# First input blocks and V weights on two DMA queues, one block's norm sums on ScalarE, the first block scaled in halves, the last two stores in another order

## The chip, the core and the metric

The kernel runs on one core of a Trainium2 chip. A core has TensorE (PE, matmuls; PEld is its loading of weights), VectorE (DVE), ScalarE (ACT), GpSimd (POOL) and SyncE (SP). Each runs its own list of instructions in a fixed order and waits for others through semaphores. SP and ACT can issue DMA transfers, each on a queue of its own. The metric is the device time of one execution in microseconds (us); five runs of the kernel before lie between 279.61 and 280.01, with a median of 279.67.

## The reference

Input `x` is 2048 rows of 512 in bf16. It is layer-normed; the normed rows feed an attention with a sliding window (32 heads of 16, each row sees itself and the 255 rows before it) and a gated product of width 1792. The output is the sum of `x` and both.

```python
xn = layernorm(x)                                   # mean and variance of each row, eps 1e-5
q, k, v = split(xn @ wqkv)                          # 32 heads, 16 wide
p = softmax(where(0 <= i - j < 256, q @ k.T * 0.25, -1e9))
a = (p @ v) @ wo
g = ((xn @ w_gate) * (xn @ w_up)) @ w_down
return x + a + g
```

## The kernel before

The 2048 rows are 16 blocks of 128 rows, four blocks to a chunk, so four chunks. `run` (L424) first calls `setup` and `first_chunk`, and then walks through 96 steps of scores (`scores`, L214: S = K Q on PE, exponential on ACT, masks on POOL). After each step it puts as many pieces of other PE work as a running account of costs allows: projections of the next chunk, gate and up products, down products, output products. The order of every engine's instructions follows from the order of these calls; nothing is reordered later. A wait is put in wherever an instruction reads what another engine wrote.

`setup` (L49) issues all loads on SP's queue, in this order: x block 0, x block 1, x blocks 2 and 3 together (L61 and L62), the three column groups of the weights for V, K and Q (L63 and L64), halves of the gate and up weights with x blocks 4 to 7 between, then the down and output weights and the rest of x. A transfer counts on one of eight completion counters in turn; the ninth waits until the counter it takes is free. ACT meanwhile loads its function table and runs one exponential on a 128x1 tile (L77). PE runs 42 products of a unit matrix (L87), whose result is not used.

`first_chunk` (L190) norms the blocks of chunk 0. For a block:

- `norm_stats` (L110): DVE makes the statistics of 512 columns (`st`, L116) and turns them into mean and variance (`mv`, L117).
- `norm_scale` (L120): POOL adds eps (`ve`, L125) and raises to the power -0.5 (`rs`, L127), both on 128x1.
- `norm_apply` (L131): DVE subtracts the mean and multiplies by `rs`, which gives `xn` (L135). The `xn` tiles come from a ring of four buffers.
- `norm_transpose` (L139): PE transposes `xn` in four pieces of 128 columns (`xTp`, L151), and ACT copies them to `xnT` (L152).
- `proj_v` (L160): four products of `xnT` with V's weights on PE (`vp`, L165), copied to `V` by ACT (L169).

In the kernel before DVE's order is: statistics of blocks 0 and 1, scaling of 0, statistics of 2, scaling of 1, statistics of 3, scaling of 2, scaling of 3. PE's order is: transposes of 0, of 1, V product of 0, transposes of 2, V product of 1, transposes of 3, V products of 2 and 3, then the first K and Q products (L177). ACT's order is `xnT` of 0 and 1, V of 0, `xnT` of 2, V of 1, `xnT` of 3, V of 2 and 3.

At the end the sum of the last block (chunk 3, block 3) lies as two halves of 256 columns in two banks of one PSUM tile, `psd3`. `wo` (L320) runs its last eight products, four for the first half and four for the second; in the second half a product with a unit matrix has already added `x` (`add_x`, L325). `store` (L331) drains a half: the second by a copy on ACT, stored from ACT's queue; the first by an addition of `x` on DVE, stored from SP's queue. Before the change the second half's `store` is called first (L485), then the first half's (L486).

Of the kernel before, what the change touches and what calls it, by code (L numbers as in the profile page):

```python
# [7 lines left out]
BF16 = mybir.dt.bfloat16  # L8
F32 = mybir.dt.float32
I32 = mybir.dt.int32  # L10
ACT = mybir.ActivationFunctionType
ALU = mybir.AluOpType
# [10 lines left out]
class Kernel:  # L23
# [25 lines left out]
    def setup(self):  # L49
        nc, const, NT, NF = self.nc, self.const, self.NT, self.NF  # L50
        self.x = const.tile([128, NT, 512], BF16, name="x")
        self.Wqkv = const.tile([128, 4, 1536], BF16, name="Wqkv")
        self.Wo = const.tile([128, 4, 512], BF16, name="Wo")
        self.Wg = const.tile([128, 4, self.F], BF16, name="Wg")
        self.Wu = const.tile([128, 4, self.F], BF16, name="Wu")
        self.Wd = const.tile([128, NF, 512], BF16, name="Wd")
        xv = self.x_d.rearrange("(t p) d -> p t d", p=128)
        wq = self.w_d["qkv"].rearrange("(k p) n -> p k n", p=128)
        wg = self.w_d["g"].rearrange("(k p) n -> p k n", p=128)
        wu = self.w_d["u"].rearrange("(k p) n -> p k n", p=128)  # L60
        for lo, hi in ((0, 1), (1, 2), (2, 4)):  # L61
            nc.sync.dma_start(out=self.x[:, lo:hi, :], in_=xv[:, lo:hi, :])  # L62
        for lo in (1024, 512, 0):  # L63
            nc.sync.dma_start(out=self.Wqkv[:, :, lo:lo + 512], in_=wq[:, :, lo:lo + 512])  # L64
        h = self.F // 2
        for lo in (0, h):
            nc.sync.dma_start(out=self.Wg[:, :, lo:lo + h], in_=wg[:, :, lo:lo + h])
            nc.sync.dma_start(out=self.Wu[:, :, lo:lo + h], in_=wu[:, :, lo:lo + h])
            if lo == 0:
                nc.sync.dma_start(out=self.x[:, 4:8, :], in_=xv[:, 4:8, :])  # L70
        nc.sync.dma_start(out=self.Wd[:], in_=self.w_d["d"].rearrange("(f p) n -> p f n", p=128))
        nc.sync.dma_start(out=self.Wo[:], in_=self.w_d["o"].rearrange("(c p) n -> p c n", p=128))
        nc.sync.dma_start(out=self.x[:, 8:NT, :], in_=xv[:, 8:NT, :])

        warm = const.tile([128, 1], F32, name="warm")
        nc.vector.memset(warm[:], 0.0)
        nc.scalar.activation(out=warm[:], in_=warm[:], func=ACT.Exp)  # L77
        ident = const.tile([128, 128], BF16, name="ident")
        nc.gpsimd.memset(ident[:], 0.0)
        nc.gpsimd.affine_select(out=ident[:], in_=ident[:], compare_op=ALU.not_equal, fill=1.0,  # L80
                                base=0, pattern=[[-1, 128]], channel_multiplier=1)
        self.ident = ident
        self.accb = self.ps_a.tile([128, 512], F32, name="accb")
        nc.vector.memset(self.accb[:], 0.0)
        wps = self.ps_m.tile([128, 128], F32, tag="M", name="wps")
        for _ in range(42):
            nc.tensor.matmul(wps[:], lhsT=ident[:], rhs=ident[:], start=True, stop=True)  # L87
        pi = const.tile([128, 1], I32, name="pi")
        nc.gpsimd.iota(pi[:], pattern=[[0, 1]], base=0, channel_multiplier=1)
        podd = const.tile([128, 1], I32, name="podd")  # L90
        nc.vector.tensor_scalar(out=podd[:], in0=pi[:], scalar1=4, scalar2=1,
                                op0=ALU.arith_shift_right, op1=ALU.bitwise_and)
        self.odd = const.tile([128, 1], F32, name="odd")
        nc.vector.tensor_copy(out=self.odd[:], in_=podd[:])
        self.mhalf = const.tile([128, 4], F32, name="mhalf")
        nc.gpsimd.memset(self.mhalf[:], -0.5)
        self.xnT, self.Q, self.hT, self.O, self.OT = {}, {}, {}, {}, {}
        self.K, self.Ko, self.V = {}, {}, {}
        self.strips, self.at = {}, {}
# [20 lines left out]
    def norm_scale(self, t, n=4):  # L120
# [7 lines left out]
        for u in range(t, t + n):  # L128
            self.stats[u][2] = rs

    def norm_apply(self, t):  # L131
        nc = self.nc
        mv, j, rs = self.stats.pop(t)
        xn = self.xpool.tile([128, 512], BF16, tag="xn", name="xn")
        nc.vector.tensor_scalar(out=xn[:], in0=self.x[:, t, :], scalar1=mv[:, j, 0:1],  # L135
                                scalar2=rs[:, j:j + 1], op0=ALU.subtract, op1=ALU.mult)
        self.xns[t] = xn

    def norm_transpose(self, t, by_dma):  # L139

        nc = self.nc
        xn = self.xns.pop(t)
        T, b = divmod(t, 4)
        if b == 0:
            self.xnT[T] = self.chunk2.tile([128, 4, 4, 128], BF16, tag="xnT", name=f"xnT{T}")
        if by_dma:
            nc.sync.dma_start_transpose(out=self.xnT[T][:, b, :, :], in_=xn[:])
            return
        ps = self.ps_m.tile([128, 4, 128], BF16, tag="M", name="xTp")
        for k in range(4):  # L150
            nc.tensor.transpose(ps[:, k, :], xn[:, 128 * k:128 * k + 128], self.ident[:])  # L151
        nc.scalar.activation(out=self.xnT[T][:, b, :, :], in_=ps[:], func=ACT.Copy)  # L152

    def bank(self, ks, name):

# [34 lines left out]
    def first_chunk(self):  # L190

        self.new_chunk(0)
        for b in range(2):
            self.norm_stats(b, 1)
            self.norm_scale(b, 1)
        for b in range(4):
            self.norm_apply(b)
            if b < 2:
                self.norm_stats(b + 2, 1)
                self.norm_scale(b + 2, 1)  # L200
        self.norm_transpose(0, False)
        for b in range(4):
            if b < 3:
                self.norm_transpose(b + 1, False)
            self.proj_v(b)
        self.proj_qk(0, 0, 1)
        self.proj_qk(0, 0, 0, on_act=True)
        self.proj_qk(0, 1, 1)
# [215 lines left out]
    def run(self):  # L424
# [49 lines left out]
        T = NCH - 1  # L474
# [7 lines left out]
        fill(10 ** 9, -1)  # L482
        assert n == len(work)
        self.wo(T, 3, (0, 1, 2, 3))
        self.store(T, 3, 1, True)  # L485
        self.store(T, 3, 0)  # L486


@with_exitstack
# [34 lines left out]
```

## Time and profile before

| | |
|---|---|
| median of five runs | 279.67 us (279.61 to 280.01) |
| the profiled execution, its own time | 279.66 us |
| its span, first to last instruction | 277.9 us |
| busy: PE, DVE, ACT, POOL | 269.1, 188.2, 183.1, 164.4 us |
| granted TensorE clock, mean | 0.999 of full speed |
| first x block landed, first statistics | 2.92 us |
| first transposes of block 0 on PE | 5.32 us |
| first V product | 6.85 us |
| first K product | 11.01 us |
| last matmuls issued from | 273.12 us, for 1.04 us |
| last store issued | 275.06 us |

The span is shorter than the time by 1.76 us, which lies around the first and the last instruction. A line of the timeline gives start and length in us, the engine, the line of the kernel, what is written and read, the shapes, and in brackets how long the engine was idle before it and what released it. `SPq` and `ACTq` are DMA issues of SP and ACT; their length is the time that the issue took, and how long a transfer took to land stands with the DMA issues. Matmuls are pipelined, so that one PE line can start before the one before it has ended.

### The profile page before, as it was taken

The page shows a single profiled execution, that of the slowest core. Times are in us where ns is not written, and L with a number is a line of the kernel's source. Part 1 is how long each engine was busy: PE and PEld are TensorE (multiplying, and loading weights), DVE is VectorE, ACT ScalarE, POOL GpSimd, SP SyncE. Part 2 cuts the span into 40 slices and gives each one's busy share as a digit, 9 for nine tenths or more (in the row PEclk, how much of TensorE's full clock was granted, in tenths as well). Part 3 has the DMA queues.
Part 4 walks back from the last instruction along what each step waited for, and adds up shares of the span by engine and source line. Part 5 has one row for each costly group of instructions (what it writes and reads, how often), then busy time and mean ns, then how long its engine had stood idle before and what let it go on. Part 6 is the DMA issues. An engine that isn't in the chain of part 4 may idle for free.

```text
span 277.9 us, 5829 instructions
## 1 busy us (share of the span) xinstructions
PE 269.1 (97%) x2396; PEld 114.4 (41%) x2414; DVE 188.2 (68%) x338; ACT 183.1 (66%) x121; POOL 164.4 (59%) x284
## 2 busy tenths in 40 slices
PE   6999999999999999999999999999999999999994
PEld 6433333334344444344444344444434444433453
DVE  6387989788567777858855778774853477777232
ACT  3666766786767666688666676769676766767601
POOL 4146666765786756574877656575656566656510
PEclk9999999999999999999999999999999999999999
DMA  7999411000112100000012200000001000000002
GB/s 215 375 371 349 110 21 21 19 0 2 39 40 57 21 2 0 1 2 0 2 40 59 55 2 2 0 2 1 0 2 40 19 21 1 2 0 2 0 2 75
DMA packets 17162, 13.74 MB, mean 49 GB/s; under 512 B 7024, under 2 KB 17136, under 8 KB 17136
## 3 DMA queue, kind: packets, MB, share of 16 engines
q1 hardware_dynamic: 16848, 13.18, 15.5%
q8 instruction: 19, 0.31, 0.5%
q10 hardware_dynamic: 288, 0.20, 0.2%
q14 instruction: 7, 0.06, 0.1%
HBM read 9.70 MB, written 2.10 MB: 42 GB/s over the span
## 4 chain that ended last, share of the span: by engine, by line
PE 87%; ACT 5%; DVE 3%; issue 1%; POOL 1%; DMA 1%; ACTq 0%; DVEq 0%
PE psd L317 18%; PE up L300 17%; PE gp L289 17%; PE S L223 11%; PE qkp L177 9%; PE accb L256 7%; PE psd L323 5%; ACT P L231 4%; PE vp L165 3%; ACT V L169 1%; DMA x<-in_A_x_dram 1%; DVE st L116 1%; DVE gsb L294 1%; DVE xn L135 1%; DVE hT L304 0%
## 5 line engine op out<-in xcount | busy, mean ns | idle before, releaser
L231 ACT ACTIVATE P<-S 128x2048 bf16<-128x2048 f32 (+2 forms) x96 | 170.0, 1771 | 74.3 <-PE S L223 62.6
L236 POOL TENSOR_SCALAR_AFFINE_SELECT P<-P 128x512 bf16<-128x512 bf16 x128 | 84.7, 662 | 54.3 <-ACT P L231 54.2
L240 POOL TENSOR_SCALAR_AFFINE_SELECT P<-P 128x512 bf16<-128x512 bf16 x112 | 72.5, 647 | 38.3 <-ACT P L231 38.3
L300 PE MATMUL up<-xnT,Wu 128*128 128x512 bf16 x224 | 60.0, 380 | 0.1
L289 PE MATMUL gp<-xnT,Wg 128*128 128x512 bf16 x224 | 59.7, 380 | 0.0
L317 PE MATMUL psd<-Wd,hT 128*128 128x512 bf16 (+1 forms) x225 | 52.3, 366 | 1.4 <-issue 1.1
L263 DVE STREAM_TRANSPOSE at<-accb 128x512 f32<-128x512 f32 x32 | 22.8, 714 | 39.0 <-PE accb L256 39.0
L304 DVE TENSOR_TENSOR hT<-up,gsb 128x512 bf16<-128x512 f32 x56 | 38.1, 681 | 7.8 <-PE up L300 5.8
L294 DVE CAST gsb<-gp 128x512 bf16<-128x512 f32 x56 | 37.9, 677 | 5.9 <-PE gp L289 5.8
L317 PEld LDWEIGHTS <-hT 128*128 128x128 bf16 x238 | 21.5, 98 | 24.9 <-issue 4.7
L289 PEld LDWEIGHTS <-Wg 128*128 128x128 bf16 x224 | 20.0, 97 | 26.1 <-issue 5.2
L177 PE MATMUL qkp<-xnT,Wqkv 128*128 128x512 bf16 x128 | 30.6, 380 | 0.0
L300 PEld LDWEIGHTS <-Wu 128*128 128x128 bf16 x224 | 19.6, 97 | 26.4 <-issue 7.1
L256 PE MATMUL accb<-P,V 128*17 128x384 bf16 (+2 forms) x704 | 25.4, 276 | 0.0
L341 DVE TENSOR_TENSOR y<-psd,x 128x512 bf16<-128x512 f32 (+1 forms) x15 | 9.9, 667 | 17.9 <-PE psd L323 16.5
L223 PE MATMUL S<-Q,K 16*128 16x256 bf16 (+2 forms) x352 | 18.4, 276 | 0.5
L223 PE MATMUL S<-Q,Ko 32*128 32x256 bf16 (+2 forms) x352 | 18.4, 275 | 0.4 <-ACT P L231 0.2
L276 DVE TENSOR_TENSOR on<-at,rz 128x256 bf16<-128x256 f32 x32 | 18.1, 566 | 0.4
L177 PEld LDWEIGHTS <-Wqkv 128*128 128x128 bf16 x128 | 11.4, 98 | 14.6 <-issue 2.7
L256 PEld LDWEIGHTS <-V 128*17 128x17 bf16 x704 | 13.8, 90 | 8.7 <-issue 5.3
L182 DVE CAST K<-qkp 128x512 bf16<-128x512 f32 x16 | 11.0, 689 | 9.0 <-PE qkp L177 8.7
L323 PE MATMUL psd<-Wo,OT 128*128 128x512 bf16 (+1 forms) x67 | 16.6, 367 | 0.2 <-issue 0.2
(39 smaller groups left out, 140.1 us busy)
## 6 DMA issues: line engine op xcount, KB each, us to landing
Wg<-in_B_w_gate_dram SPq DMA_DIRECT2D x2, 896.0 KB, 10.3
Wu<-in_B_w_up_dram SPq DMA_DIRECT2D x2, 896.0 KB, 11.5
Wd<-in_B_w_down_dram SPq DMA_DIRECT2D x1, 1792.0 KB, 15.5
out_dram<-y SPq DMA_DIRECT2D x14, 128.0 KB, 1.7
Wqkv<-in_A_wqkv_dram SPq DMA_DIRECT2D x3, 512.0 KB, 5.8
x<-in_A_x_dram SPq DMA_DIRECT2D x1, 1024.0 KB, 10.4
x<-in_A_x_dram SPq DMA_DIRECT2D x1, 512.0 KB, 10.9
Wo<-in_A_wo_dram SPq DMA_DIRECT2D x1, 512.0 KB, 15.4
```

The costliest lines, as they stand in the source:

```text
L177: nc.tensor.matmul(ps[:], lhsT=self.Wqkv[:, k, lo:lo + 128], rhs=self.xnT[T][:, :, k, :], start=(k == 0), stop=(k == 3))
L223: nc.tensor.matmul(S[:, e, col:col + n], lhsT=(self.Ko if par else self.K)[U][rows, c, 128 * j:128 * j + 128], rhs=self.Q[T][rows, c, 128 ...
L231: nc.scalar.activation(out=P[:, :, lo:hi], in_=S[:, :, lo:hi], func=ACT.Exp, scale=0.25)
L236: nc.gpsimd.affine_select(out=P[:, :, j:j + 128], in_=P[:, :, j:j + 128], pattern=[[0, 4], [1, 128]], compare_op=ALU.is_ge, fill=0.0, base ...
L240: nc.gpsimd.affine_select(out=P[:, :, j:j + 128], in_=P[:, :, j:j + 128], pattern=[[0, 4], [-1, 128]], compare_op=ALU.is_gt, fill=0.0, bas ...
L256: nc.tensor.matmul(acc[32 * e:32 * e + 17, 128 * q0:128 * q0 + n], lhsT=self.V[U][:, v, 8 * c + 2 * e + par, 0:17], rhs=P[:, e, col:col + ...
L289: nc.tensor.matmul(ps[:], lhsT=self.Wg[:, k, 128 * f:128 * f + 128], rhs=self.xnT[T][:, :, k, :], start=(k == 0), stop=(k == 3))
L294: nc.vector.tensor_copy(out=self.gsb[:], in_=ps[:])
L300: nc.tensor.matmul(ps[:], lhsT=self.Wu[:, k, 128 * f:128 * f + 128], rhs=self.xnT[T][:, :, k, :], start=(k == 0), stop=(k == 3))
L304: nc.vector.tensor_tensor(out=self.hT[T][:, f, :], in0=ps[:], in1=self.gsb[:], op=ALU.mult)
L317: nc.tensor.matmul(ps, lhsT=self.hT[T][:, f, 128 * b:128 * b + 128], rhs=self.Wd[:, f, c0:c1], start=(f == 0), stop=False)
L323: self.nc.tensor.matmul(ps, lhsT=self.OT[T][:, c, 128 * b:128 * b + 128], rhs=self.Wo[:, c, c0:c1], start=False, stop=(c == 3))
```

## The change

- x blocks 0 and 2 are loaded from SP's queue, 1 and 3 from ACT's, one transfer each. V's weights are loaded in two halves by rows: SP takes the first, ACT the second. K's and Q's follow on SP.
- Block 3's statistics are no longer made on DVE. ACT makes two passes over it, a copy and a square, each with a sum over the columns; POOL makes mean and variance of the sums with four instructions on 128x1 (`norm_stats_act`). The two passes' full outputs go to two `xn` buffers that nobody reads.
- Block 0 is scaled in two halves of 256 columns, and transposed and copied in two halves too, each with a PSUM tile of its own.
- DVE's order is now: statistics of 0 and 1, scaling of 0, statistics of 2, scaling of 1, 2 and 3. POOL's order is: `ve` and `rs` of blocks 0 and 1, the four instructions for block 3, `ve` and `rs` of block 2, then of block 3. PE's order is unchanged, apart from block 0's halves.
- At the end the first half's `store` is called before the second half's.

```diff
-        for lo, hi in ((0, 1), (1, 2), (2, 4)):
-            nc.sync.dma_start(out=self.x[:, lo:hi, :], in_=xv[:, lo:hi, :])
-        for lo in (1024, 512, 0):
+        for b in range(4):
+            (nc.scalar if b % 2 else nc.sync).dma_start(out=self.x[:, b, :], in_=xv[:, b, :])
+        for k in (0, 2):
+            (nc.scalar if k else nc.sync).dma_start(out=self.Wqkv[:, k:k + 2, 1024:1536], in_=wq[:, k:k + 2, 1024:1536])
+        for lo in (512, 0):
             nc.sync.dma_start(out=self.Wqkv[:, :, lo:lo + 512], in_=wq[:, :, lo:lo + 512])
...
+    def norm_stats_act(self, t):
+
+        nc = self.nc
+        sums = self.small.tile([128, 2], F32, tag="sums", name="sums")
+        for j, func in enumerate((ACT.Copy, ACT.Square)):
+            junk = self.xpool.tile([128, 512], BF16, tag="xn", name="junk")
+            nc.scalar.activation(out=junk[:], in_=self.x[:, t, :], func=func, accum_out=sums[:, j:j + 1])
+        mv = self.small.tile([128, 1, 2], F32, tag="mv", name="mv")
+        mean, sq = mv[:, 0, 0:1], self.small.tile([128, 2], F32, tag="sq", name="sq")
+        nc.gpsimd.tensor_scalar(out=mean, in0=sums[:, 0:1], scalar1=1.0 / 512, scalar2=None, op0=ALU.mult)
+        nc.gpsimd.tensor_scalar(out=sq[:, 0:1], in0=sums[:, 1:2], scalar1=1.0 / 512, scalar2=None, op0=ALU.mult)
+        nc.gpsimd.tensor_tensor(out=sq[:, 1:2], in0=mean, in1=mean, op=ALU.mult)
+        nc.gpsimd.tensor_tensor(out=mv[:, 0, 1:2], in0=sq[:, 0:1], in1=sq[:, 1:2], op=ALU.subtract)
+        self.stats[t] = [mv, 0, None]
+
     def norm_apply(self, t):
...
-        nc.vector.tensor_scalar(out=xn[:], in0=self.x[:, t, :], scalar1=mv[:, j, 0:1],
-                                scalar2=rs[:, j:j + 1], op0=ALU.subtract, op1=ALU.mult)
+        for c0, c1 in ((0, 256), (256, 512)) if t == 0 else ((0, 512),):
+            nc.vector.tensor_scalar(out=xn[:, c0:c1], in0=self.x[:, t, c0:c1], scalar1=mv[:, j, 0:1],
+                                    scalar2=rs[:, j:j + 1], op0=ALU.subtract, op1=ALU.mult)
...
-        ps = self.ps_m.tile([128, 4, 128], BF16, tag="M", name="xTp")
-        for k in range(4):
-            nc.tensor.transpose(ps[:, k, :], xn[:, 128 * k:128 * k + 128], self.ident[:])
-        nc.scalar.activation(out=self.xnT[T][:, b, :, :], in_=ps[:], func=ACT.Copy)
+        for k0, k1 in ((0, 2), (2, 4)) if t == 0 else ((0, 4),):
+            ps = self.ps_m.tile([128, 4, 128], BF16, tag="M", name="xTp")
+            for k in range(k0, k1):
+                nc.tensor.transpose(ps[:, k, :], xn[:, 128 * k:128 * k + 128], self.ident[:])
+            nc.scalar.activation(out=self.xnT[T][:, b, k0:k1, :], in_=ps[:, k0:k1, :], func=ACT.Copy)
...
-        for b in range(2):
+        for b in (0, 1):
             self.norm_stats(b, 1)
             self.norm_scale(b, 1)
-        for b in range(4):
+        self.norm_stats_act(3)
+        self.norm_apply(0)
+        self.norm_stats(2, 1)
+        self.norm_scale(2, 1)
+        self.norm_scale(3, 1)
+        for b in (1, 2, 3):
             self.norm_apply(b)
-            if b < 2:
-                self.norm_stats(b + 2, 1)
-                self.norm_scale(b + 2, 1)
         self.norm_transpose(0, False)
...
         self.wo(T, 3, (0, 1, 2, 3))
+        self.store(T, 3, 0)
         self.store(T, 3, 1, True)
-        self.store(T, 3, 0)
```

## The prediction

> **What bounds the kernel now.** I read the page first (busy shares and the chain that ended last), then the timeline of the first 14 us, where all but one of the edits lie, then the issues and landings of single DMAs and the busy windows there, and last the timeline of the end.
>
> ```profile
> PE 269.1 (97%) x2396; PEld 114.4 (41%) x2414; DVE 188.2 (68%) x338; ACT 183.1 (66%) x121; POOL 164.4 (59%) x284
> PE 87%; ACT 5%; DVE 3%; issue 1%; POOL 1%; DMA 1%; ACTq 0%; DVEq 0%
> ```
>
> PE is busy 97% of the span and is 87% of the chain. From the first projection on its fixed order runs nearly without a gap, so a shift of that beginning moves the end by as much. What the edits can win or lose lies in the chain before PE is full, and in the 3.7 us after its last matmul.
>
> ```profile
> 2.92 0.69 DVE L116 BATCH_NORM_STATS2 st<-x 128x6 f32<-128x512 bf16 x1 [1.08 <-DMA x<-in_A_x_dram]
> 4.85 0.41 DVE L135 TENSOR_SCALAR xn<-x,mv,rs 128x512 bf16<-128x512 bf16 x1 [0.22 <-POOL rs L127]
> 5.09 0.60 POOL L127 TENSOR_TENSOR rs<-ve,mhalf 128x1 f32<-128x1 f32 x1
> 5.99 0.38 DVE L135 TENSOR_SCALAR xn<-x,mv,rs 128x512 bf16<-128x512 bf16 x1
> 6.17 0.29 POOL L125 TENSOR_SCALAR ve<-mv 128x1 f32<-128x1 f32 x1 [0.48 <-DVE mv L117]
> 6.43 0.40 PE L151 MATMUL xTp<-ident,xn 128*128 128x128 bf16 x4 [0.72 <-DVE xn L135]
> 6.54 0.57 POOL L127 TENSOR_TENSOR rs<-ve,mhalf 128x1 f32<-128x1 f32 x1
> 6.82 0.56 PEld L165 LDWEIGHTS <-xnT 128*128 128x128 bf16 x4 [0.16 <-issue]
> 7.14 0.41 DVE L135 TENSOR_SCALAR xn<-x,mv,rs 128x512 bf16<-128x512 bf16 x1
> 7.71 0.39 PE L151 MATMUL xTp<-ident,xn 128*128 128x128 bf16 x4
> 7.93 1.03 PE L165 MATMUL vp<-Wqkv,xnT 128*128 128x512 bf16 x4
> ```
>
> The timeline: start, length, engine, line. The first x block lands at 2.92. Block 1's transposes wait on DVE until 6.43. The first V product follows at 6.82, though PE's weight loads were free at 6.66. Block 2's transposes (7.71) only follow that product: their input was scaled by 7.55. POOL is free for 0.48 us before block 2's `ve`; that hole is the whole slack ahead of block 2.
>
> ```profile
> x<-in_A_x_dram SPq DMA_DIRECT2D x1, 256.0 KB, 2.9
> Wqkv<-in_A_wqkv_dram SPq DMA_DIRECT2D x1, 512.0 KB, 4.5
> ...
> 2.00:4.00 2.00, 2.00 (x22) 2.00 (x20) 1.04 (x3) 0.28 (x2) 0.08 (x1) 1.00 0.94 236
> ```
>
> V's weights, issued at 2.20, land 4.5 later, at 6.7: they are what held the first V product. The third line is the busy window of 2 to 4 us: the DMA engines are 94% busy (last but one column), at 236 GB/s.
>
> ```profile
> 273.12 1.04 PE L323 MATMUL psd<-Wo,OT 128*128 128x256 bf16 x8
> 274.19 0.38 ACT L339 ACTIVATE y<-psd 128x256 bf16<-128x256 f32 x1 [1.47 <-PE psd L323]
> 274.60 0.34 ACTq L342 DMA_DIRECT2D out_dram<-y  x1
> 274.61 0.42 DVE L341 TENSOR_TENSOR y<-psd,x 128x256 bf16<-128x256 f32 x1 [1.42 <-ACT y L339]
> ```
>
> At the end the halves of the last sum are drained one after the other: ACT's half, and then DVE's, which waited for ACT's though its own matmuls had ended earlier.
>
> **The change part by part.** Times are those of this execution: span 277.9, 279.66 us with what lies around it, 0.01 below the median of 279.67.
>
> *First x blocks on two queues.* SP now issues x0, x2; ACT x1, x3. SP's first issue is at 0.81 and ACT is free from 0.80, so x0 and x1 start together, where x0 was alone. Nothing stood ahead of x0 before, so it can't land earlier: at least 0. At most it waits for all of x1: 128 KB at 236 GB/s = 0.55. The nearest rows are the stores at the end: SP's at 272.62 lands in 1.7, the median of its 14, and ACT's, issued 0.13 later beside it, in 2.0. The first loses 0 and the second 0.3; which of x0 and x1 is first is open, so I take half: +0.15 on the chain.
>
> The Trainium skill, "DMA: Bandwidth & Descriptors", section "Issuing engines are not separate DMA queues", speaks against this edit: transfers from several engines interleave on the same DMA engines, and only the sequencer's issue time is saved. The 94% of the window agrees. By that rule, sharing evenly, x0 would come up to 0.55 late and the sum below would be 280.7; by the stores' rows it is 280.3.
>
> *V's weights in two halves.* V needs the same 1 MB moved as before, now without waiting for four issues (0.4 to 0.5 each) in one queue: between 6.7 and some 0.8 earlier. The first V product then hangs on block 1's transposes, not on the weights: at most 0.16 won, swallowed below. K's and Q's weights come earlier too, to no use: they land by 10.0 and are first used near 11. Wg's first issue now reuses a completion counter and waits for x1's landing, some 0.2; its product starts at 19.05, its data lands near 12.4.
>
> *ACT's queue.* Three issues (some 0.42 each) now stand ahead of the table load (1.28): it ends near 3.4 instead of 2.08, the warm-up near 3.6. The two sums of block 3 wait for x3, which lands between 3.4 (as x1 did) and 4.63 (as blocks 2 and 3 did). A 128x512 pass costs 0.60 from PSUM, 128x1 from SBUF 0.20; with 0.6 each they end between 4.8 and 5.85. Behind them on ACT stands block 0's copy, now two of 0.38 for one of 0.60: done by 6.6 at the latest, before the V product at 6.8. The second tile of block 0 moves the ring of three PSUM buffers on by one: the first V product takes the buffer of block 0's first half, copied out by then. The sums are hidden, or 0.15 past the 5.69 at which POOL asks for them; from an early x3 they stay hidden up to 1.1 each. Their unused outputs take two of the four `xn` buffers, so blocks 2 and 3 are scaled only after them, which they are anyhow.
>
> *DVE.* Block 3's statistics (0.69 + 0.18) go; they stood beside POOL's work for block 2 and cost nothing. Block 0 in two halves adds one instruction's start, between 0.06 (a 128x1 memset on DVE) and 0.18 (the aggregation), 0.1 taken; a gain is excluded, since the bytes stay the same. Block 2's statistics stand ahead of block 1's scaling as before. That scaling moves from 5.99 to 6.09, its transposes to 6.53, the V product to 6.76: 0.06 better than 6.82.
>
> *POOL: the step that decides.* Four new instructions on 128x1 stand after block 1's `rs` (ends 5.69) and ahead of block 2's `ve`. Floor: a 128x1 memset, 0.10: four and one dependent wait of 0.09 (3.92 + 0.23 to 4.24) are 0.49, as long as the hole of 0.48: nothing lost, and no gain, since `ve` waits for its statistics. Ceiling: 0.35 (the dearest `ve`) for the two scalings, 0.57 (`rs`, a power) for the two with two inputs: 1.93, block 2 late by 1.43. Nearest is `ve` itself, a 128x1 arithmetic instruction, mean 0.24 over 16: 4 x 0.24 + 0.09 = 1.05, to 6.74. Then `ve` 0.29 to 7.03, wait 0.09, `rs` 0.57 to 7.69, 0.04, scaling 0.41 to 8.14, and block 2's transposes 0.06 later, 8.20 against 7.71: **+0.49**. PE stands idle for it (its V product ends at 7.62), so the 0.06 won above goes there. Block 3's `ve` and `rs` end near 8.6, its scaling at 9.04; its transposes come after the second V product at 9.28, so nothing more is lost. What follows keeps its distances: ACT alternates V copies and transposed blocks as before.
>
> *The end.* The built program's waits show no overlap gained: DVE's store waits for the count that PE reaches with its very last matmul, and ACT's store now waits for DVE's. 0.38 + 0.04 + 0.42 becomes 0.42 + 0.04 + 0.38; then ACT issues (0.34) instead of SP (0.33), both land in 1.6. 0, within 0.1.
>
> **Sum:** 0.15 + 0.49 + 0 = +0.64 on 279.66: **280.3 us**.
>
> **The rivals.**
> (B) *Hidden after all.* POOL's four instructions cost near 0.10, not 0.24, as memsets and the iota (0.13) do, and x0 is served first. Block 2 stays at its place: 279.6 to 280.1. It decides where the four together stay below about 0.9. For it: the hole of 0.48. Against: no arithmetic row of POOL is under 0.22.
> (C) *Sums late.* A sum on ACT costs 1.2, as two passes would: from 4.63 they end at 7.0. POOL's chain starts 1.3 later than 5.69, and block 2's transposes come at 9.5: +1.8, 281.5 at the worst; with x3 at 3.8 it is +1.0, 280.7. For it: no row shows a summing pass. Against: x3 can land earlier.
> (D) *The edits do what they say.* The first half is drained while the second is summed: 0.42 off the end, and 0.16 from V's weights if block 2 is in time as well: 279.1. Against it stand the waits named above, and it wants both.
>
> **How the numbers follow.** The bound of what can be told apart is 0.2%, 0.56 us: 279.11 and 280.23. My case (280.0 to 280.8) 0.55, of it 0.13 under the bound; B 0.28; C 0.13, all slower; D 0.04. Slower: 0.42 + 0.13 = 0.55. Same: 0.13 + 0.28 = 0.41. Faster: 0.04. The range leaves out D, the cheapest part of B and the dearest of C: 279.8 to 281.0.
>
> **What would show it.** After the change: POOL with six instructions in a row between block 1's and block 2's scaling, and no hole before block 2's `ve`; PE idle by 0.3 to 0.7 before block 2's transposes, put down to DVE's scaling; the first statistics starting at 2.9 to 3.4; the first V product no longer behind its weights; at the end DVE before ACT, at the same sum. I am wrong if block 2's transposes follow the first V product without a gap, if ACT's sums end after 5.7, or if the two last drains overlap.

## The result and the profile after

| | before | after |
|---|---|---|
| median of all runs | 279.94 us (95 runs) | 280.45 us (53 runs) |
| ratio to before, 95% interval | | 1.0023 (1.0018 to 1.0029) |
| the profiled execution, its own time | 279.66 us | 280.55 us |
| its span | 277.9 us | 278.9 us |
| first statistics (x block 0 landed) | 2.92 | 3.43 |
| first V product | 6.85 | 8.01 |
| block 2's scaling ends / its transposes start | 7.55 / 7.71 | 8.52 / 8.87 |
| first K product | 11.01 | 12.17 |
| last products of the kernel start | 273.12 | 274.28 |
| last store issued | 275.06 | 276.23 |

The change costs 0.23%, which is 0.64 us on 279.94 (0.50 to 0.81 by the interval). The ratio goes by the means, and five of after's 53 executions, against one of before's 95, took 282 us or more; the medians differ by 0.51 us. The prediction had the same sum, but two of its terms were wrong, and their errors are larger than that agreement suggests. Over 95 runs the median of before is 0.28 us above its profiled execution.

From the page of the changed kernel, the busy times:

```profile
PE 269.7 (97%) x2396; PEld 115.1 (41%) x2414; DVE 187.7 (67%) x337; ACT 184.5 (66%) x126; POOL 165.0 (59%) x288
```

PE still binds, with as many instructions as before. From the first K product to the kernel's last products both executions take 262.11 us (273.12 - 11.01 and 274.28 - 12.17), so that all of the 1.16 us by which the last products are late was lost before 12.17. The timeline of the changed kernel there:

```profile
0.80 0.90 ACTq L62 DMA_DIRECT2D x<-in_A_x_dram  x2
0.80 0.88 SPq L62 DMA_DIRECT2D x<-in_A_x_dram  x2
...
3.43 0.69 DVE L118 BATCH_NORM_STATS2 st<-x 128x6 f32<-128x512 bf16 x1 [1.59 <-DMA x<-in_A_x_dram]
4.42 0.63 ACT L139 ACTIVATE junk<-x 128x512 bf16<-128x512 bf16 x1 [0.70 <-DMA x<-in_A_x_dram]
4.96 0.19 ACT L139 ACTIVATION_READ_ACCUMULATOR junk<-x 128x1 f32 x1
...
5.57 0.19 ACT L139 ACTIVATION_READ_ACCUMULATOR junk<-x 128x1 f32 x1
5.60 0.57 POOL L129 TENSOR_TENSOR rs<-ve,mhalf 128x1 f32<-128x1 f32 x1
6.26 0.24 POOL L142 TENSOR_SCALAR mv<-sums 128x1 f32<-128x1 f32 x1
6.46 0.21 POOL L143 TENSOR_SCALAR sq<-sums 128x1 f32<-128x1 f32 x1
6.63 0.19 POOL L144 TENSOR_TENSOR sq<-mv 128x1 f32<-128x1 f32 x1
6.69 0.38 DVE L153 TENSOR_SCALAR xn<-x,mv,rs 128x512 bf16<-128x512 bf16 x1
6.90 0.22 POOL L145 TENSOR_TENSOR mv<-sq 128x1 f32<-128x1 f32 x1
7.13 0.40 PE L170 MATMUL xTp<-ident,xn 128*128 128x128 bf16 x4 [0.83 <-DVE xn L153]
7.21 0.21 POOL L127 TENSOR_SCALAR ve<-mv 128x1 f32<-128x1 f32 x1
7.50 0.57 POOL L129 TENSOR_TENSOR rs<-ve,mhalf 128x1 f32<-128x1 f32 x1
8.01 1.02 PE L184 MATMUL vp<-Wqkv,xnT 128*128 128x512 bf16 x3 [0.49 <-DMA Wqkv<-in_A_wqkv_dram]
8.11 0.41 DVE L153 TENSOR_SCALAR xn<-x,mv,rs 128x512 bf16<-128x512 bf16 x1 [1.04 <-POOL rs L129]
8.87 0.39 PE L170 MATMUL xTp<-ident,xn 128*128 128x128 bf16 x4
```

Three things stand in it. The first statistics wait for x block 0 until 3.43, 0.51 later than before. POOL makes six instructions in a row from 6.26 and ends block 2's `rs` at 8.07. And the first V product waits for V's weights (its bracket), while block 2's transposes follow that product without an idle bracket. Block 2's transposes need both: their scaled input, and PE free of the V product. Both chains are late, and the later one sets 8.87:

- Block 2: scaled at 8.52, so transposes could start at 8.58, with the 0.06 between e.g. 8.34 and 8.40 in run 1 below.
- V: with the weights in early, the product starts 0.23 after block 1's transposes, as in run 1 below (6.91 - 6.68). In before that would have been 6.66; it started at 6.85, 0.19 late, 0.14 after its weights had landed. In after it would have been 7.36 = 6.66 + 0.51 (x block 0) + 0.19 (the halves of block 0). It started at 8.01: 0.65 late by the weights. Transposes follow 0.86 behind a V product, as before (7.71 - 6.85): 8.87.

So V's weights came last, 0.29 behind block 2's scaling, and in place of the weights' gain there is a loss. The same from the DMA issues of the changed kernel between 1.73 and 2.2 us (queue, count, KB, us from issue to landing):

```profile
Wqkv<-in_A_wqkv_dram SPq DMA_DIRECT2D x1, 256.0 KB, 6.1
Wqkv<-in_A_wqkv_dram ACTq DMA_DIRECT2D x1, 256.0 KB, 6.3
```

And from its chain of waits in the first 12 us (start, length, what), of which this piece is 51%:

```profile
1.73 6.15 DMA Wqkv<-in_A_wqkv_dram
```

Each half holds half of what was 512 KB in 4.5 us, was issued up to 0.5 us earlier than that transfer, and took longer: in at 7.88 and 8.06 where the whole was in by 6.71. The end of the changed kernel:

```profile
274.28 1.04 PE L344 MATMUL psd<-Wo,OT 128*128 128x256 bf16 x8
275.36 0.42 DVE L362 TENSOR_TENSOR y<-psd,x 128x256 bf16<-128x256 f32 x1 [1.00 <-PE psd L344]
275.82 0.38 ACT L360 ACTIVATE y<-psd 128x256 bf16<-128x256 f32 x1 [1.93 <-DMA out_dram<-y]
276.23 0.35 ACTq L363 DMA_DIRECT2D out_dram<-y  x1
```

The first half's drain starts only after the last of all eight products, and ACT's copy only after DVE's addition. From the last products to the last issue it is 1.95 us, against 1.94. ACT's bracket names an older store; ACT starts 0.04 after DVE is done.

One part of the account stays without a cause: from the start of the last products to the end of the execution's own time are 6.54 us before and 6.27 after (280.55 - 274.28). The own times therefore differ by 0.89 us, not 1.16. Runs 2 and 5 below share this (6.24, 6.32), and the other two-queue runs, 7 and 11, do not (6.50, 6.56). The order of the last stores isn't it: run 3, with the changed end, has 6.68.

### The profile page after: what moved, and what is told of

Same layout as the page of the kernel before. It is cut to its first block, busy times and chain, and to the rows that moved or that the text cites. A ratio compares the mean times of both kernels' runs of the same rounds, so it can differ in the third digit from the quotient of the medians.

```text
span 278.9 us, 5840 instructions
## 1 busy us (share of the span) xinstructions
PE 269.7 (97%) x2396; PEld 115.1 (41%) x2414; DVE 187.7 (67%) x337; ACT 184.5 (66%) x126; POOL 165.0 (59%) x288
## 4 chain that ended last, share of the span: by engine, by line
PE 86%; ACT 5%; DMA 3%; DVE 2%; issue 1%; POOL 1%; SPq 0%; ACTq 0%; DVEq 0%
PE psd L338 17%; PE up L321 17%; PE gp L310 17%; PE S L244 10%; PE qkp L196 9%; PE accb L277 7%; PE psd L344 5%; ACT P L252 4%; PE vp L184 3%; DMA Wqkv<-in_A_wqkv_dram 2%; ACT V L188 1%; DMA out_dram<-y 1%; DVE gsb L315 1%; DVE hT L325 0%; POOL P L257 0%
```

## The experiments

All kernels compute the whole result. Times are medians with before's beside them, then the ratio with its 95% interval; stages are of the profiled execution. "V" is the start of the first V product, "tr. 2" that of block 2's transposes, "K" of the first K product. The medians differ by less than the K columns do from the profiled execution of before (11.01), whose time lies low among its runs: run 3, whose beginning is before's, has 11.22.

| run | median / before, us | ratio | x block 0 | V | tr. 2 | K |
|---|---|---|---|---|---|---|
| before | | | 2.92 | 6.85 | 7.71 | 11.01 |
| after | 280.45 / 279.94 | 1.0023 (1.0018 to 1.0029) | 3.43 | 8.01 | 8.87 | 12.17 |
| 1, old loads | 280.49 / 280.00 | 1.0019 (1.0010 to 1.0028) | 2.98 | 6.91 | 8.40 | 11.71 |
| 2, new loads alone | 280.63 / 280.00 | 1.0025 (1.0016 to 1.0033) | 3.63 | 7.81 | 8.67 | 11.97 |
| 3, new end alone | 280.04 / 280.00 | 1.0013 (0.9997 to 1.0029) | 2.98 | 7.06 | 7.92 | 11.22 |
| 4, sums alone | 280.29 / 280.00 | 1.0015 (1.0006 to 1.0024) | 2.96 | 6.84 | 8.53 | 11.84 |
| 5, x alone on two queues | 280.65 / 280.03 | 1.0026 (1.0010 to 1.0041) | 3.35 | 8.16 | 9.02 | 12.32 |
| 6, V alone on two queues | 279.97 / 280.03 | 1.0000 (0.9991 to 1.0009) | 3.23 | 7.21 | 8.16 | 11.47 |
| 7, after, later loads held back | 280.62 / 280.03 | 1.0027 (1.0017 to 1.0036) | 3.57 | 7.50 | 8.72 | 12.03 |
| 8, four POOL steps after block 2 | 280.59 / 280.03 | 1.0024 (1.0015 to 1.0033) | 2.94 | 6.87 | 7.82 | 11.77 |
| 8b, two POOL steps after block 2 | 280.07 / 280.01 | 1.0003 (0.9995 to 1.0012) | 3.00 | 6.93 | 7.88 | 11.29 |
| 9, end in two tiles | 279.46 / 280.01 | 0.9988 (0.9979 to 0.9996) | 2.92 | 6.79 | 7.65 | 10.95 |
| 10, run 9 with V before x block 3 | 279.85 / 280.01 | 1.0001 (0.9990 to 1.0011) | 3.00 | 7.20 | 8.39 | 11.70 |
| 11, run 5, later loads held back | 280.21 / 279.85 | 1.0011 (1.0002 to 1.0021) | 3.64 | 7.38 | 8.33 | 11.64 |

In every row PE takes 261.9 to 262.4 us from the first K product to the kernel's last products. What the beginning loses is paid in full.

### Runs 1 to 4: the change taken apart

Run 1, against after:

```diff
-        for b in range(4):
-            (nc.scalar if b % 2 else nc.sync).dma_start(out=self.x[:, b, :], in_=xv[:, b, :])
-        for k in (0, 2):
-            (nc.scalar if k else nc.sync).dma_start(out=self.Wqkv[:, k:k + 2, 1024:1536], in_=wq[:, k:k + 2, 1024:1536])
-        for lo in (512, 0):
+        for lo, hi in ((0, 1), (1, 2), (2, 4)):
+            nc.sync.dma_start(out=self.x[:, lo:hi, :], in_=xv[:, lo:hi, :])
+        for lo in (1024, 512, 0):
```

> The changed kernel with its loads put back as they were before; the sums on ACT, the halves of block 0 and the order at the end stay. Theory W (the loads are the cost: with two queues V's weights land at 8.0 instead of 6.7): the first V product comes back to 6.8 to 6.9 us, and what is left is POOL's chain. Theory P (POOL's four instructions are a cost of their own, hidden in the changed kernel behind the late weights): block 2's transposes come at 8.2 to 8.5 instead of 7.71, PE waits 0.5 to 0.8 for them, and the time is 0.4 to 0.8 us above before. If P is wrong and only the loads cost anything: within 0.1 us of before. If instead the loads are harmless and the rest costs all: as slow as the changed kernel, V product at 8.0.

Run 2 is before with the lines that run 1 takes out of after:

```diff
-        for lo, hi in ((0, 1), (1, 2), (2, 4)):
-            nc.sync.dma_start(out=self.x[:, lo:hi, :], in_=xv[:, lo:hi, :])
-        for lo in (1024, 512, 0):
+        for b in range(4):
+            (nc.scalar if b % 2 else nc.sync).dma_start(out=self.x[:, b, :], in_=xv[:, b, :])
+        for k in (0, 2):
+            (nc.scalar if k else nc.sync).dma_start(out=self.Wqkv[:, k:k + 2, 1024:1536], in_=wq[:, k:k + 2, 1024:1536])
+        for lo in (512, 0):
```

> The kernel before with the loads of the changed kernel alone. Theory W: x0 lands at 3.4 instead of 2.92, V's weights at 7.5 to 8.1 instead of 6.7, the first V product at 7.6 to 8.1, and all that follows is late by as much as it is: first K product 11.8 to 12.2, time 0.5 to 1.1 us above before, the whole of the change's loss. Rival (the late weights come from ACT's sums or from POOL, or were a chance of one execution): V product at 7.3 at most, time at most 0.4 above.

Run 3, against before:

```diff
         self.wo(T, 3, (0, 1, 2, 3))
-        self.store(T, 3, 1, True)
         self.store(T, 3, 0)
+        self.store(T, 3, 1, True)
```

> The kernel before with the two last stores in the other order. My working: both drains wait for PE's last matmul and for each other, so DVE then ACT (0.42 + 0.38) takes the place of ACT then DVE, and the time stays within 0.1 us. Rival (the halves are drained as they finish): the first drain starts 0.4 to 0.5 before PE's end, and 0.4 us is won.

Run 4 is before with `norm_stats_act` as in the change, called in the changed order, and block 0 whole:

```diff
-        for b in range(4):
+        self.norm_stats_act(3)
+        self.norm_apply(0)
+        self.norm_stats(2, 1)
+        self.norm_scale(2, 1)
+        self.norm_scale(3, 1)
+        for b in (1, 2, 3):
             self.norm_apply(b)
-            if b < 2:
-                self.norm_stats(b + 2, 1)
-                self.norm_scale(b + 2, 1)
```

> The kernel before with block 3's sums on ACT and the new order of DVE and POOL, without the halves, the loads or the order at the end. Here x block 3 lands near 4.66 with block 2, and the two passes with their readings take 1.35 us together (measured in the changed kernel: 0.54 + 0.19 + 0.52 + 0.19 from start to start), so POOL gets the sums near 6.1. Theory P: POOL's four instructions (0.86 there) end near 7.0, block 2 is scaled by 8.3 to 8.4, its transposes at 8.3 to 8.5 instead of 7.71, time 0.5 to 0.8 above before. Rival (POOL's instructions stay beside other work): block 2's transposes at 7.9 at most, time within 0.2.

The loads alone and the rest alone each cost about as much as everything: K moves by 0.96 with the loads (run 2), by 0.70 without them (run 1), by 1.16 with both. The two losses lie beside each other for the most part, as the two chains in the profile say. Timeline of run 1:

```profile
6.24 0.21 POOL L141 TENSOR_SCALAR sq<-sums 128x1 f32<-128x1 f32 x1 [0.19 <-ACT junk L137]
...
6.68 0.40 PE L168 MATMUL xTp<-ident,xn 128*128 128x128 bf16 x4 [0.48 <-DVE xn L151]
...
6.91 1.03 PE L182 MATMUL vp<-Wqkv,xnT 128*128 128x512 bf16 x3
...
7.93 0.41 DVE L151 TENSOR_SCALAR xn<-x,mv,rs 128x512 bf16<-128x512 bf16 x1 [1.31 <-POOL rs L127]
...
8.40 0.40 PE L168 MATMUL xTp<-ident,xn 128*128 128x128 bf16 x4 [0.46 <-DVE xn L151]
```

With the old loads V is at its old place, and PE now stands idle for 0.46 before block 2's transposes, put down to DVE's scaling, which waited for POOL: the picture that the prediction drew. POOL's stretch from block 1's `rs` to block 2's `ve` is 1.32 us here (5.71 to 7.03), against 1.05 forecast and 1.04 in after: blocks 2 and 3 are one transfer again, ACT's second sum ended only at 6.15, and POOL waited for it. So POOL did wait for the sums, by 0.28, as rival C feared; but the cause is the late landing, and not a pass that costs 1.2: a pass is 0.63. In run 4 another thing made POOL late: x block 1's statistics waited for their load until 4.09 (3.75 before), although no load was touched. Two of that transfer's 16 parts landed at 4.05 and 4.07, the other 14 by 3.28. So a landing on SP's queue alone can differ by 0.7 us between executions (3.39 in before).

Timeline of run 2:

```profile
3.63 0.69 DVE L118 BATCH_NORM_STATS2 st<-x 128x6 f32<-128x512 bf16 x1 [1.79 <-DMA x<-in_A_x_dram]
...
7.81 1.02 PE L167 MATMUL vp<-Wqkv,xnT 128*128 128x512 bf16 x3 [0.27 <-DMA Wqkv<-in_A_wqkv_dram]
```

Both halves of the loads' loss without any of the sums. Run 3's medians agree within 0.04 us and its interval takes in 1; the timeline of its end shows the changed kernel's waits:

```profile
274.40 0.42 DVE L341 TENSOR_TENSOR y<-psd,x 128x256 bf16<-128x256 f32 x1 [1.00 <-PE psd L323]
...
274.85 0.38 ACT L339 ACTIVATE y<-psd 128x256 bf16<-128x256 f32 x1 [1.93 <-DMA out_dram<-y]
275.27 0.34 ACTq L342 DMA_DIRECT2D out_dram<-y  x1
```

Its last products start at 273.32: 1.95 to the last issue. The end is worth nothing either way.

### Runs 5, 6, 7 and 11: why V's weights came late

Run 5 is before with x on two queues and V whole on SP; run 6 is before with only V in halves:

```diff
-        for lo, hi in ((0, 1), (1, 2), (2, 4)):
-            nc.sync.dma_start(out=self.x[:, lo:hi, :], in_=xv[:, lo:hi, :])
+        for b in range(4):
+            (nc.scalar if b % 2 else nc.sync).dma_start(out=self.x[:, b, :], in_=xv[:, b, :])
```

> The kernel before, with the first four x blocks alternating between SP's and ACT's queue; V's weights whole and alone on SP, as before. Theory S (a transfer that shares the DMA engines with one of the other queue is slowed, the first as much as the second): x0 lands at 3.3 to 3.5; V's weights, which share only with what is left of x, land at 6.3 to 6.9; the V product starts at 7.0 to 7.3, bound by block 1's transposes; first K product 11.2 to 11.5, time 0.2 to 0.5 us above before. Rival (any use of both queues delays the weights): V product at 7.6 or later, as with all loads changed.

```diff
-        for lo in (1024, 512, 0):
+        for k in (0, 2):
+            (nc.scalar if k else nc.sync).dma_start(out=self.Wqkv[:, k:k + 2, 1024:1536], in_=wq[:, k:k + 2, 1024:1536])
+        for lo in (512, 0):
```

> The kernel before, with V's weights alone in two halves; x stays on SP, so that ACT issues its half at 0.8 us, beside x0. Theory S: x0 shares with ACT's half and lands at 3.2 to 3.5, x2 and x3 at 5.0 or later; ACT's half is in early, SP's half follows x and shares with nothing of ACT's by then, so V is complete at 6.3 to 7.0 and the V product starts at 6.9 to 7.4; time 0.1 to 0.5 above before. Rival (splitting V is itself the cost): V complete at 7.5 or later and 0.6 or more above.

Run 7 is after, with K's and Q's weights and all later loads moved behind block 1's statistics; a small copy of these on SP's queue makes the queue wait for them, so that the loads are issued from 5.9:

```diff
-        for lo in (512, 0):
-            nc.sync.dma_start(out=self.Wqkv[:, :, lo:lo + 512], in_=wq[:, :, lo:lo + 512])
...
+    def late_loads(self):
...
+        nc.sync.dma_start(out=self.gate_t[:], in_=self.stats[1][0][:, 0, :])
+        for lo in (512, 0):
+            nc.sync.dma_start(out=self.Wqkv[:, :, lo:lo + 512], in_=wq[:, :, lo:lo + 512])
...
             self.norm_scale(b, 1)
+        self.late_loads()
```

> The changed kernel, but K's, Q's and all later weights are issued only after block 1's statistics, near 5.2 us, behind a small transfer of those statistics; until then nothing but x and V's weights is on the two queues. Theory C (V's weights are late because K's weights, behind the smaller half on SP, take turns with ACT's half on the same engines): V lands at 6.0 to 6.9, V product at 7.0 to 7.3 (block 1's transposes), and block 2's scaling, which POOL sets, becomes the next wait, transposes near 8.5; time 0.3 to 0.8 above before. Rival S2 (the two queues are slow by themselves, or some engines straggle): V lands at 7.5 or later as in the changed kernel.

Run 11 is run 5 with the same `late_loads`, and V whole on SP ahead of them (against before):

```diff
...
+        for b in range(4):
+            (nc.scalar if b % 2 else nc.sync).dma_start(out=self.x[:, b, :], in_=xv[:, b, :])
+        nc.sync.dma_start(out=self.Wqkv[:, :, 1024:1536], in_=wq[:, :, 1024:1536])
...
             self.norm_scale(b, 1)
+        self.late_loads()
```

> As the run with the x blocks alone on two queues, where V's weights came late at 8.0 (fourteen of their sixteen parts by 6.1, the last two at 7.04 and 8.04), but K's, Q's and all later weights are issued only after block 1's statistics. Theory C2 (the last parts of V are late when much is issued behind them in the same queue while the other queue is in use): all of V is in by 6.1 to 6.6, the V product starts at 7.0 to 7.3, and with POOL's chain as before the first K product is at 11.2 to 11.5, time 0.1 to 0.4 above before. Rival S3 (two queues at the start leave one or two DMA engines slow whatever follows): the last parts at 7.0 or later again, V product at 7.2 or later, first K product at 11.6 or later.

In run 5 V's weights are one transfer on SP, as before, and yet the V product waits longest of all (timeline of run 5):

```profile
8.16 1.02 PE L165 MATMUL vp<-Wqkv,xnT 128*128 128x512 bf16 x4 [0.91 <-DMA Wqkv<-in_A_wqkv_dram]
```

So the halves aren't the cause, and theory S, which had the weights in by 6.9, was wrong. A transfer is recorded as landing in 16 parts; of these 14 had landed by 6.09 and the last two at 7.02 and 8.03. In after the last parts are late too: 11 of the 16 parts of SP's half are in by 5.84 and the last at 7.88, 10 of ACT's half by 6.60 and the last at 8.06. In run 6 x is on SP alone and ACT's half of V has its queue to itself. It is in at 3.95, and SP's half at 6.70, no earlier than the whole was. ACT's half by the DMA issues of run 6 (KB, us to landing):

```profile
Wqkv<-in_A_wqkv_dram ACTq DMA_DIRECT2D x1, 256.0 KB, 3.2
```

Run 6's x block 0 is late too (3.23): ACT's half of V is issued beside it at 0.80, as x block 1 is in after, and theory S had said so (3.2 to 3.5). Its K is 0.25 behind run 3's, but its time is that of before, where 0.1 to 0.5 more was expected. With the later loads held back, the two V halves of run 7 take, by its DMA issues (KB, us from issue to landing):

```profile
Wqkv<-in_A_wqkv_dram SPq DMA_DIRECT2D x1, 256.0 KB, 4.7
Wqkv<-in_A_wqkv_dram ACTq DMA_DIRECT2D x1, 256.0 KB, 4.9
```

And the one transfer of run 11, by the same view:

```profile
Wqkv<-in_A_wqkv_dram SPq DMA_DIRECT2D x1, 512.0 KB, 4.9
```

They are in by 6.42 and 6.60 in run 7, and by 6.64 in run 11: 1.4 us earlier than in after and run 5. Run 11's V product (7.38) and K lie in rival S3's ranges all the same, but by x block 0 (3.64) and not by the weights: the product starts 0.23 behind block 1's transposes at 7.15. Together the four runs show that V is late where x uses both queues and much is issued behind V, and not where either is absent. All profiled executions agree, one of each kernel: V is complete at 7.88 to 8.06 in after and runs 2 and 5, at 6.60 and 6.64 in runs 7 and 11, and at 6.40 to 6.92 in the nine with x on SP alone. What they don't show is why single parts fall behind in that case; late single parts come on SP's queue alone as well, at other transfers (x block 1 in run 4; K's weights in run 8, 15 parts by 8.04 and the last at 9.15). My reading before run 5, "K's weights take turns with ACT's half", doesn't cover V whole on SP, and is not shown.

Run 7 is also the cleanest measure of the prediction's two terms, for V is out of the way (timeline):

```profile
7.50 1.03 PE L193 MATMUL vp<-Wqkv,xnT 128*128 128x512 bf16 x4
...
8.72 0.40 PE L179 MATMUL xTp<-ident,xn 128*128 128x128 bf16 x4 [0.19 <-DVE xn L162]
```

Block 2 is scaled at 8.66, 1.11 behind before: x block 0 gives 0.65 (3.57 - 2.92), POOL the other 0.46. K is 1.02 late and the ratio 1.0027. Taking V's lateness away saved 0.14 at K and nothing in the time, since block 2 held PE instead (and x block 0 came 0.14 later than in after). In run 11, where neither V's weights nor POOL's steps are in the way, x block 0 alone remains: 0.72 at the first statistics, 0.63 at K, and 0.11% (0.02 to 0.21).

### Runs 8 and 8b: POOL's four instructions behind block 2

Both have the old loads. Run 8 is run 1 with the four POOL instructions in a function of their own, called after block 2's `ve` and `rs`; run 8b makes them two, as ACT's passes already scale by 1/512 and 512 to the power -0.5:

```diff
         self.norm_scale(2, 1)
+        self.norm_stats_pool(3)
         self.norm_scale(3, 1)
```

> The kernel with the loads as before and all other edits, with POOL's four instructions for block 3 put after block 2's two instead of ahead of them. Theory P (each instruction on POOL stands in a chain without slack): block 2's transposes come back to 7.7 to 7.95 from 8.40; but now block 3 waits, its scaling ends at 9.2 to 9.5 and its transposes come 0.4 to 0.7 after the second V product has ended, so that the first K product stays at 11.4 to 11.8 and the time 0.3 to 0.7 above before: moving the four does not help. Rival (block 2's lateness came from ACT's sums alone): block 3's transposes follow the V product without a gap and the first K product is at 11.1 or earlier.

```diff
-        for j, func in enumerate((ACT.Copy, ACT.Square)):
+        for j, (func, scale) in enumerate(((ACT.Copy, 1.0 / 512), (ACT.Square, 512 ** -0.5))):
...
-        nc.gpsimd.tensor_scalar(out=mean, in0=sums[:, 0:1], scalar1=1.0 / 512, scalar2=None, op0=ALU.mult)
-        nc.gpsimd.tensor_scalar(out=sq[:, 0:1], in0=sums[:, 1:2], scalar1=1.0 / 512, scalar2=None, op0=ALU.mult)
-        nc.gpsimd.tensor_tensor(out=sq[:, 1:2], in0=mean, in1=mean, op=ALU.mult)
-        nc.gpsimd.tensor_tensor(out=mv[:, 0, 1:2], in0=sq[:, 0:1], in1=sq[:, 1:2], op=ALU.subtract)
+        nc.gpsimd.tensor_tensor(out=sq[:], in0=sums[:, 0:1], in1=sums[:, 0:1], op=ALU.mult)
+        nc.gpsimd.tensor_tensor(out=mv[:, 0, 1:2], in0=sums[:, 1:2], in1=sq[:], op=ALU.subtract)
```

> As the run with POOL's instructions after block 2's, but ACT's passes scale by 1/512 and by its root, so that their sums are mean and mean square, and POOL has two instructions instead of four. Theory P: 0.4 to 0.5 us less for POOL before block 3's scaling, which ends near 8.8 to 9.0; block 3's transposes wait 0.2 at most, first K product 11.1 to 11.4, time within 0.3 of before. If POOL is not what block 3 waits for: no change against that run.

Timeline of run 8, the transposes of blocks 2 and 3 with block 3's scaling between:

```profile
7.82 0.40 PE L172 MATMUL xTp<-ident,xn 128*128 128x128 bf16 x4
...
9.34 0.41 DVE L155 TENSOR_SCALAR xn<-x,mv,rs 128x512 bf16<-128x512 bf16 x1 [1.58 <-POOL rs L127]
...
9.81 0.40 PE L172 MATMUL xTp<-ident,xn 128*128 128x128 bf16 x4 [0.73 <-DVE xn L155]
```

Timeline of run 8b, block 3's transposes:

```profile
9.34 0.40 PE L171 MATMUL xTp<-ident,xn 128*128 128x128 bf16 x4 [0.19 <-DVE xn L154]
```

In run 8 block 2's transposes come without a gap after the V product, and block 3's are late instead, with PE idle for 0.73: K is at 11.77, where run 1 had 11.71. (Block 3 was scaled at 9.75, 0.25 past the expected range.) Moving the work only moved the wait. Two instructions fewer bring block 3's transposes forward by 0.47, two at 0.24 each, and the time back to before's. In run 8b block 3 was scaled at 9.28, 0.3 to 0.5 later than expected.

### Runs 9 and 10: an end that does overlap

In run 9 the second half of the last sum lies in a PSUM tile of its own, and its down products lag those of the first half by four. The first half is stored first:

```diff
-                self.sums[b] = [(four[:, 0, 0:256], 0, 256), (four[:, 1, 0:256], 256, 512)]
+                self.sums[b] = [(four[:, 0, 0:256], 0, 256), (self.accb[:, 0:256], 256, 512)]
...
-        for f in range(lo, hi):
-            for ps, c0, c1 in self.sums[b]:
+        for p, (ps, c0, c1) in enumerate(self.sums[b]):
+            for f in range(lo, hi) if p == 0 else range(max(0, lo - 4), hi - 4 if hi < self.NF else hi):
...
-        self.store(T, 3, 1, True)
         self.store(T, 3, 0)
+        self.store(T, 3, 1, True)
```

> The kernel before with the last sum's halves in two PSUM tiles instead of two banks of one: the second half goes to the tile of the attention sums, which is free by then, and its down products run two pairs behind the first half's; the first half's store is called first. Theory E (the two drains waited for PE's last product and for each other only because they read one tile): DVE drains the first half while PE finishes the second, ACT starts at PE's end, the last issue comes 0.42 to 0.48 earlier after PE's last product than before, time 0.3 to 0.5 us below before. Rival (the end is bound by the stores' landing or by what follows it): no more than 0.1 won.

The end in the timeline of run 9:

```profile
273.05 0.60 PE L323 MATMUL psd<-Wo,OT 128*128 128x256 bf16 x4
273.49 0.60 PE L323 MATMUL accb<-Wo,OT 128*128 128x256 bf16 x4
273.69 0.42 DVE L341 TENSOR_TENSOR y<-psd,x 128x256 bf16<-128x256 f32 x1 [1.00 <-PE psd L323]
...
274.13 0.38 ACT L339 ACTIVATE y<-accb 128x256 bf16<-128x256 f32 x1 [1.91 <-DMA out_dram<-y]
274.54 0.34 ACTq L342 DMA_DIRECT2D out_dram<-y  x1
```

DVE drains the first half from 273.69, while PE works at `accb` to 274.09; ACT drains the second from 274.13. Beside the order of the stores, which alone is worth nothing (run 3), two things were changed at once here, the tile and the lag of the down products, and they were not tried apart. The last eight products come as they did before, four for the first half and then four for the second, in 1.04 us, so that the lag does not show in them; that the tile does it is likely, and not shown. From the last products to the last issue it is 1.49 us instead of 1.94. The time falls by 0.12% (0.04% to 0.21%): this kernel is faster than the one before the change, and it is the only one here. It is what rival D had in mind, at 0.45 us.

Run 10 adds to it the loads x block 0, 1, 2, V, x block 3 on SP, to have V's weights earlier:

```diff
-        for lo, hi in ((0, 1), (1, 2), (2, 4)):
+        for lo, hi in ((0, 1), (1, 2), (2, 3)):
             nc.sync.dma_start(out=self.x[:, lo:hi, :], in_=xv[:, lo:hi, :])
...
+            if lo == 1024:
+                nc.sync.dma_start(out=self.x[:, 3:4, :], in_=xv[:, 3:4, :])
```

> As the run with two tiles at the end, and x block 3 loaded after V's weights instead of before, all on SP's queue. Theory: V's weights land 0.3 earlier, at 6.3 to 6.5, the V product starts at 6.66 to 6.75, at once behind block 1's transposes; x3 lands near 6.7, its statistics wait for it 0.4, and block 3's transposes wait 0.1 to 0.3 in turn, which gives back as much: within 0.2 of the run with two tiles alone. If block 3 has slack: another 0.1 to 0.2 won.

DVE in the timeline of run 10, x block 3's statistics and block 2's scaling:

```profile
7.12 0.70 DVE L118 BATCH_NORM_STATS2 st<-x 128x6 f32<-128x512 bf16 x1 [0.68 <-DMA x<-in_A_x_dram]
...
7.95 0.38 DVE L137 TENSOR_SCALAR xn<-x,mv,rs 128x512 bf16<-128x512 bf16 x1
```

A miss. V's weights were in at 6.72 as before, and x block 3 came so late that its statistics, which stand ahead of block 2's scaling on DVE, held it to 7.95. What the end had won was lost again.

## Why the prediction was right and where it was wrong

- **Direction and sum: right.** +0.64 forecast from the profiled execution's 279.66, +0.64 by the ratio, +0.51 by the medians. The agreement to the hundredth is chance: x block 0 and the weights were put too low, and against them stand the 0.27 that went after the last products, and a profiled execution of before that lies 0.28 under its median.
- **Its signs of being wrong: two of three came.** Block 2's transposes follow the first V product without a gap, and ACT's sums end at 5.76, after 5.7. The two last drains do not overlap. Of the signs of being right, the first V product was to be free of its weights and was not. So the path that the prediction named, POOL ahead of block 2, is not the one that set after's beginning: it was done 0.29 earlier than the weights' chain. The 1.16 at K are 0.51 (x block 0), 0.19 (the halves of block 0) and 0.46 (the weights, 0.65 - 0.19), and nothing of POOL's; that the sum held all the same is luck.
- **POOL, "the step that decides": its size was right, its place not.** Forecast were 1.05 from `rs` to `ve` and +0.49 for block 2. Measured are 1.04 in after, and +0.46 in after and in run 7 once x block 0's delay is taken off (8.52 - 7.55 - 0.51). The four busy times are 0.24, 0.21, 0.19 and 0.22, close to the 0.24 of the row that I took, for products of two inputs as for scalings. The forecast's sign of it, PE idle before block 2's transposes and put down to DVE, is not in after, where the V product covers it; it is in runs 1, 4 and 7 (0.46, 0.65, 0.19), where the weights are in time.
- **x on two queues: the mis-sized term.** "I take half: +0.15" measured +0.51 in after, and +0.43 to +0.72 over the five kernels with x on both queues (3.35 to 3.64), against 2.92 to 3.00 in the eight with the first loads on SP alone, and 3.23 in run 6. The bound of 0.55, one whole block at 236 GB/s, was the better guess, and no ceiling: three of the five lie above it. I let two stores at the end of the kernel set the value, when nothing else was on the DMA engines, although the window of 2 to 4 us was 94% busy. The Trainium skill, "DMA: Bandwidth & Descriptors", section "Issuing engines are not separate DMA queues", says that the transfers interleave on the same engines and that only issue time is saved. These runs agree: no x block 0 came earlier. The section states no price; the 0.55 was my estimate by even sharing, and the price in after is 0.51.
- **V's weights: the step that failed.** "Between 6.7 and some 0.8 earlier", and "the first V product then hangs on block 1's transposes, not on the weights". The halves landed 1.17 and 1.35 later than the whole, the product waited 0.65 for them (0.19 before), and 0.29 of that reached PE beyond POOL's chain. I had counted bytes ahead of V in the queues, and not what stood behind it: runs 7 and 11 show that without those later loads the two queues have V complete at 6.60 and 6.64, the late edge of my bounds, and there is no gain in any.
- **The sums on ACT: right in after.** A pass took 0.63, and a separate reading of the sum 0.19, unforeseen; both passes ended at 5.76, inside 4.8 to 5.85. POOL asked at 6.26, since it was late itself. POOL waited only with the old loads: by 0.28 in run 1, and by less than 0.1 in run 4.
- **Block 0 in halves: too low.** +0.1 was taken; block 1's scaling starts 3.26 behind the first statistics, against 3.07 before: +0.19, just past the upper bound of 0.18. It lay under the wait for the weights. No run has the halves alone.
- **The end: right.** 1.95 against 1.94, and run 3 alone is no slower. A drain runs beside the last products only in runs 9 and 10, where the halves have tiles of their own.

## What to carry to other kernels

Where the DMA engines are near full (94% busy here), putting the first load and its successor on two queues can delay the load that everything waits for, here by 0.43 to 0.72 us, and a third transfer's landing may depend on what is issued behind it. So look at the engines' busy share before counting queue positions. When two chains meet at one engine, cost both: taking out the one that shows in the brackets (V's weights in run 7) won nothing in the time, because the other stood right behind it. And the reorder of the stores bought no overlap here, with both halves in one tile; a tile for each half, with the down products of the second lagging, did.

## What the runs showed that I had not expected

- 512 KB of V's weights, issued at about the same time, were complete 4.2 to 4.9 us after their issue with x on SP alone or with nothing behind them, and 5.9 to 6.3 with x on two queues and the later loads issued at once. In run 5 it was two parts of 16 that took the last 1.9 us (6.09 to 8.03). Why single parts fall behind is open.
- With two queues the DMA engines moved more at first and less after that. The busy window of 2 to 4 us of after shows a share of 0.98 and 273 GB/s (last two columns), where before had 0.94 and 236; that of 4 to 5.3 us 0.76 and 216, where before had 0.89 and 298 by the same view. Over both windows that is some 827 KB against 859:

```profile
2.00:4.00 2.00, 2.00 (x22) 2.00 (x20) 0.57 (x1) 1.49 (x2) 0.00 (x0) 1.00 0.98 273
4.00:5.30 1.30, 1.30 (x16) 1.30 (x15) 1.07 (x4) 0.88 (x3) 0.79 (x3) 1.00 0.76 216
```

- A sum over the columns on ACT is two instructions in the profile: the pass, 0.63 for 128x512, and 0.19 for the reading of the sum.
- The length from the first K product to the last products is the same in all kernels, 261.9 to 262.4 us, whatever came before it: there is no slack in it that takes up a late start.
